# Full 128-row transposes with masked blocks added in PSUM, and new durations in the list schedule's table

## The chip, the cores and the metric

One Trainium2 chip; the kernel runs on one of its cores. The metric is device time in microseconds (us) from the start to the end of one execution; lower is better. Several executions are made, and their median is compared. The engines are named as the profile names them: PE (TensorE matmuls), PEld (the weight loads of TensorE, which stand in a row of their own), DVE (VectorE), ACT (ScalarE), POOL (GpSimd), SP (the engine that issues the DMAs).

## The reference

Sliding-window attention with a linear bias, followed by a feed-forward layer with an unusual gate. Inputs are float32.

```python
# attention: q, k, v are (8 batches, 8 heads, 576 positions, 64)
scores = q @ k.T / sqrt(64)
rel    = pos_q - pos_k
bias   = -slope[head] * abs(rel)
scores = where((rel >= 0) & (rel < 128), scores + bias, -1e9)
attn   = exp(scores - max); attn /= attn.sum() + 1e-9
x      = (attn @ v)  # laid out as (4608 tokens, 512)

# feed-forward: w_in (512, 2048), w_out (2048, 512)
h   = x @ w_in
g   = h * erf(softplus(h))
out = g @ w_out
```

A query sees the 128 keys up to its own position. With key blocks of 64, the queries that see key block b are the 192 from 64b on.

## The kernel before, in words

The work has two halves that run interleaved. **Attention** goes over 32 pairs of heads (8 batches, 4 pairs). **The feed-forward layer**, called MoE in the code, goes over 12 chunks of 384 tokens and 16 slices of 128 hidden features, in two passes: the first pass does 6 slices for all chunks, while attention still makes the tokens, and the second does the other 10, once the memory of attention is free. A float32 product is made of three products of a rounded high part and a remainder (names ending in `h` and `l`).

One pair of heads has five query tiles (`QTILES`, line 56): four of 128 rows, and a last one of 64 rows (queries 512 to 575). For each tile, `scores` (line 472) makes the scores of both heads on PE (line 506), DVE adds the bias with the mask and takes the minimum (line 517), ACT takes the exponential and its sum (line 527); `normalise` (line 536) takes the reciprocal of the sums on DVE (lines 544, 545) and scales the tile on POOL (line 555). The result `p` has queries on partitions and, for each of up to four key blocks, 64 keys of both heads side by side (128 columns). Masked entries are exact zeros there.

The product with v needs keys on partitions, so `transpose_bank` (line 562) transposes blocks of `p` on PE into one PSUM bank (line 574), and ACT or DVE copies the bank to SBUF (lines 468, 470; `pa`, `pb`). `SPANS` (line 61) says which blocks go where: span 0 holds tiles 0 to 2 and has two banks, span 1 holds tiles 3 and 4 and has two more. An entry `(tile, r0, r1, key block)` transposes rows r0 to r1 of one key block. Since key block b is seen by 192 queries, it takes a whole tile (128 rows) and half of a neighbouring one (64 rows): the half with the mask's zeros is left out. So in a bank transposes of 128 and of 64 rows alternate: 128, 64, 128, 64, 128 in the first bank of span 0; 64, 128, 64, 128, 64 in the second; 128, 64 and 64, 64, 128, 64, 64 in those of span 1. That is 17 transposes for a pair of heads and 544 in all. `av` (line 586) then multiplies by v (line 592) into `px`, which goes to SBUF and DRAM as the tokens `x`.

MoE work on PE is line 778 (x by w_in, 384 columns) and line 840 (g by w_out, 512 columns). Lines 807 to 825 and 762, 764 make the gate on ACT, DVE and POOL.

What sets the order of the work: every piece is an `op` with a cost for each engine that may run it and a due time. `Plan.run` is a list scheduler in Python: it plays the whole program through with those costs, gives each engine the ready piece that is due first, chooses between engines where two are allowed (a copy on ACT or DVE, a remainder on DVE or POOL), and writes the instructions out in the order that results. On the chip each engine works through its list in that order. The costs are formulas in the number of columns (`f32r_us`, `fp32_us`, `dve`, `act`, `pool_tt`, `pool_ts`, lines 290 to 311). They set the order, and nothing else.

Of the kernel before, what the change touches and what calls it, by code (L numbers as in the profile page):

```python
# [25 lines left out]
CH = 384  # L26
# [26 lines left out]
W2A, W2B = 60, 2.0  # L53


QTILES = [(128, 2, 4), (128, 0, 4), (128, 0, 4), (128, 0, 4), (64, 0, 3)]

# [3 lines left out]
SPANS = [  # L61
    (
        (0, 1, 2), 0, 384,
        [
            ([(0, 0, 128, 2), (1, 0, 64, 0), (1, 0, 128, 2), (2, 0, 64, 0), (2, 0, 128, 2)], 0, 0),
            ([(0, 64, 128, 3), (1, 0, 128, 1), (1, 64, 128, 3), (2, 0, 128, 1), (2, 64, 128, 3)], 1, 0),
        ],
        {0: (0, 0, 0, 192), 2: (0, 192, 128, 320), 4: (0, 384, 256, 384),
         1: (1, 0, 64, 256), 3: (1, 192, 192, 384), 5: (1, 384, 320, 384)},
        [(0, 3), (1, 2), (4, 5)],  # L70
    ),
    (
        (3, 4), 384, S,
        [
            ([(3, 0, 128, 1), (3, 64, 128, 3)], 0, 0),
            ([(4, 0, 64, 1), (3, 0, 64, 0), (3, 0, 128, 2), (4, 0, 64, 0), (4, 0, 64, 2)], 0, 192),
        ],
        {5: (0, 0, 384, 512), 7: (0, 128, 448, 576), 4: (0, 256, 384, 448),
         6: (0, 320, 384, 576), 8: (0, 512, 512, 576)},
        [(6, 4), (5, 7, 8)],  # L80
    ),
]
SUB = ALU.subtract
# [204 lines left out]


def f32r_us(n):  # L290
    return max(n / 2400.0, 0.091) + 0.0025


def fp32_us(n):
    return max(n / 600.0, 0.191) + 0.0045


def dve(n, fast=False):
    return 0.068 + n * (0.000521 if fast else 0.001042)


def act(n, aps=0, src=0.093):
    return src + 0.093 * aps + n * 0.000833


def pool_tt(n):
    return 0.09 + n * 0.0022


def pool_ts(n):  # L310
    return 0.245 + n * 0.00083
# [27 lines left out]
class Attention:  # L339
# [132 lines left out]
    def scores(self, i, t, operands, low, total, at):  # L472
        nc, op = self.nc, self.plan.op
        g = self.order[i][1]
        m, c0, c1 = QTILES[t]
        n = (c1 - c0) * 64
        a, kh, kl, q0, k0 = operands
        q0 = t * P - q0
        k0 = (2 * t - 2 + c0) * 64 - k0
        src = []  # L480
        if kl is None:

# [6 lines left out]
            def products(e):  # L489
# [22 lines left out]
        pt = Buf(self.pp, [P, 4, 2, 64], F32, "p", PB, f"p{i}_{t}")  # L512
# [16 lines left out]
                    accum_out=total[:m, j : j + 1],  # L529
                )  # L530

        op({"DVE": 2 * dve(n)}, biased, r=list(dict.fromkeys(s[0] for s in src)), w=[pt, low], at=at)
        op({"Act": 2 * act(n, 2)}, exps, r=[pt, low], w=[pt, total], at=at)
        return pt

    def normalise(self, i, ts, p, st, totals, at):

        nc, op = self.nc, self.plan.op
        m = QTILES[ts[0]][0]
        k = [2 * (t % 3) for t in ts]  # L540
        both = lambda: st[:m, 6 + k[0] : 8 + k[-1]]

        def inverse(e):
            nc.vector.tensor_scalar(both(), both(), 1e-9, None, op0=ALU.add)
            nc.vector.reciprocal(both(), both())  # L545

        sums = [totals[t] for t in ts]
        op({"DVE": 0.28}, inverse, r=sums, w=sums, at=at)
        for t in ts:
            _, c0, c1 = QTILES[t]  # L550

            def scaled(e, t=t, c0=c0, c1=c1):
                for j in range(2):
                    dst = p[t][:m, c0:c1, j, :]
                    nc.gpsimd.tensor_scalar(  # L555
                        dst, dst, totals[t][:m, j : j + 1], 1.0, op0=ALU.mult, op1=ALU.mult
                    )

            n = (c1 - c0) * 64
            op({"Pool": 2 * (0.245 + n * 0.00083)}, scaled, r=[p[t], totals[t]], w=[p[t]], at=at)  # L560

    def transpose_bank(self, i, w, bi, p, sb, at):
        nc, op = self.nc, self.plan.op
        parts, sbi, off = SPANS[w][3][bi]
# [4 lines left out]
        width = sum(r1 - r0 for _, r0, r1, _ in parts)  # L569

        def transposes(e):
            col = 0
            for t, r0, r1, kb in parts:
                nc.tensor.transpose(  # L574
                    ps[:, col : col + r1 - r0], p[t][r0:r1, kb].rearrange("p j d -> p (j d)"),
                    self.ident[r0:r1, r0:r1],
                )
                col += r1 - r0

        op({"PE": width / 1200.0 + 0.02}, transposes,  # L580
           r=[p[t] for t in sorted({x[0] for x in parts})], w=[ps], at=at)
        op({"DVE": dve(width), "Act": act(width, src=0.051)},
           lambda e: self.copy(e, sb[sbi][:, off : off + width], ps[:, :width]),
           r=[ps], w=[sb[sbi]], at=at)

    def av(self, i, w, blks, dst, v, sb, at):
# [14 lines left out]
    def span(self, i, w, operands, v):  # L601
        b, g = self.order[i]
        op = self.plan.op
# [30 lines left out]
        op({"DVE": dve(n), "Act": act(n, src=0.051)},  # L634
           lambda e: self.copy(e, xs.all, px[:, :n]), r=[px], w=[xs], at=at + 0.1)
        xd = Part(self.moe.x_dram[c], slice(None), g, slice(off, off + n))
        self.moe.x_parts[c].append(xd)
# [55 lines left out]
class Moe:  # L693
# [72 lines left out]
    def unit(self, c, f, w, x, po, start, end, first, at):  # L766
        nc, op = self.nc, self.plan.op
        U = self.U
        wh, wl = w.t[0, f]
        ps = Buf(self.ps_h, [P, 512], F32, "h", 2, f"h{U}")  # L770
        for k2 in range(2):
            xh, xl = x[k2]

            def products(e, k2=k2, xh=xh, xl=xl):
                for k in range(2):
                    cs = slice((2 * k2 + k) * P, (2 * k2 + k + 1) * P)
                    for n, (ww, xx) in enumerate(((wh, xh), (wh, xl), (wl, xh))):
                        nc.tensor.matmul(  # L778
                            ps[:, :CH], lhsT=ww[:, cs], rhs=xx[:, k],
                            start=(k2 + k + n == 0), stop=(k2 + k + n == 4),  # L780
                        )
# [5 lines left out]
        op({"Act": act(CH, src=0.051), "DVE": dve(CH)},  # L787
           lambda e: self.copy(e, hs[:, half], ps[:, :CH]), r=[ps], w=[hs], at=at)
        return dict(U=U, c=c, f=f, w=w, po=po, start=start, end=end, first=first, hs=hs, at=at)

# [58 lines left out]
    def store(self, u, t, po, at):  # L849
# [114 lines left out]
```

## Time and profile before

| what | value |
|---|---|
| median of 3 executions | 1168.37 us (1168.31 to 1174.0) |
| the profiled execution | 1174.66 us, span 1172.9 us from first to last instruction |
| busy: PE, DVE, ACT, POOL | 97%, 62%, 58%, 33% of the span |
| mean clock granted to TensorE | 0.978 |
| transposes (line 574) | 544, the first at 14.7 us, the last at 572.9 us |

The profile is one execution. A row of a group gives busy time, the mean length of one instruction in ns, and the idle time of the engine ahead of it. A row of the timeline gives the start, the length, the engine and the instructions that were merged into it; since matmuls overlap, the time that one holds PE is the distance from its start to the start of the next, not its length. Shapes are written as rows*columns of the array, then partitions x elements.

### The profile page before, as it was taken

Reading aid. Unit: us, or ns where it says so; the run is one execution under the profiler, and the core shown is the slowest. Engines: PE = TensorE matmul, PEld = TensorE weight load, DVE = VectorE, ACT = ScalarE, POOL = GpSimd, SP = SyncE. Lnnn points to the kernel's source line nnn. Section 1 sums busy time; section 2 is a strip of 40 time slices with the busy share of each in tenths; the row PEclk is TensorE's granted clock in tenths of the full one; section 3 lists DMA queues with packets and bytes.
Section 4 is the critical chain, followed back from the end, with each engine's and each line's share of the span. In section 5 each row is a group of like instructions: output and inputs, shape, how many; then the busy total and the mean of one; then the engine's idle time right before and its main releaser. Section 6 shows DMA issues by size and latency. Waiting matters only on the chain.

```text
span 1172.9 us, 17108 instructions
## 1 busy us (share of the span) xinstructions
PE 1133.4 (97%) x6000; PEld 983.7 (84%) x6000; DVE 723.9 (62%) x1670; ACT 680.9 (58%) x1368; POOL 389.9 (33%) x464
## 2 busy tenths in 40 slices
PE   8997889999999999999999999999999999999998
PEld 6875768888778788887899999899999999999997
DVE  7877999876966686766587877343344234324433
ACT  6556656774776576756557666354455544554552
POOL 6876677636544554553333343000000000000000
PEclk9987989999998999999999999999999999999999
DMA  7443555444434234341133341122022112102102
GB/s 201 125 123 93 149 144 155 136 124 109 125 110 134 71 111 143 102 120 67 65 110 124 126 144 55 54 81 81 1 82 81 33 49 81 57 25 82 54 1 81
DMA packets 89733, 111.61 MB, mean 95 GB/s; under 512 B 45744, under 2 KB 59696, under 8 KB 89648
## 3 DMA queue, kind: packets, MB, share of 16 engines
q1 hardware_dynamic: 89648, 110.52, 31.4%
q8 instruction: 48, 0.79, 0.3%
q14 instruction: 37, 0.30, 0.1%
HBM read 82.18 MB, written 28.31 MB: 94 GB/s over the span
## 4 chain that ended last, share of the span: by engine, by line
PE 48%; DVE 1%; ACT 1%; POOL 1%; issue 0%; POOLq 0%
PE o L840 24%; PE h L778 24%; POOL wto L682 0%; DVE hs L820 0%; DVE wto L671 0%; DVE gl L825 0%; ACT s L807 0%; DVE wqo L674 0%; POOL wlo L688 0%; ACT L807 0%; DVE wqo L673 0%; PE px L592 0%; DVE wto L669 0%; DVE xl L755 0%; DVE gh L764 0%
## 5 line engine op out<-in xcount | busy, mean ns | idle before, releaser
L778 PE MATMUL h<-xh,whi 128*128 128x384 f32 x768 | 264.3, 344 | 0.0
L778 PE MATMUL h<-xh,wli 128*128 128x384 f32 x768 | 261.1, 340 | 0.4 <-POOL wli L688 0.4
L778 PE MATMUL h<-xl,whi 128*128 128x384 f32 x768 | 260.2, 339 | 0.8 <-DVE xl L755 0.8
L555 POOL TENSOR_SCALAR p<-p,st 128x256 f32<-128x256 f32 (+2 forms) x320 | 199.8, 641 | 180.3 <-DVE st L545 128.9
L840 PE MATMUL o<-who,gh 128*128 128x512 f32 x576 | 228.4, 397 | 0.0
L840 PE MATMUL o<-wlo,gh 128*128 128x512 f32 x576 | 227.8, 395 | 0.5 <-POOL wlo L688 0.5
L840 PE MATMUL o<-who,gl 128*128 128x512 f32 x576 | 228.1, 396 | 0.0
L762 ACT COPY hs<-h 128x384 f32<-128x384 f32 x142 | 67.9, 479 | 254.9 <-PE h L778 254.1
L527 ACT ACTIVATE p<-p,st 128x256 f32<-128x256 f32 (+2 forms) x320 | 149.2, 468 | 63.9 <-DVE st L517 62.9
L778 PEld LDWEIGHTS h<-xh,whi 128*128 128x128 f32 x768 | 145.9, 190 | 8.4
L778 PEld LDWEIGHTS h<-xl,whi 128*128 128x128 f32 x768 | 145.7, 190 | 7.8 <-DVE xl L755 1.1
L778 PEld LDWEIGHTS h<-xh,wli 128*128 128x128 f32 x768 | 145.4, 189 | 1.2 <-POOL wli L688 1.2
L574 PE MATMUL t<-ident,p 64*128 64x64 f32 (+1 forms) x544 | 123.7, 290 | 17.5 <-POOL p L555 14.6
L517 DVE CUSTOM_DVE_ANT_0 p<-s,bias_sb 128x256 f32<-128x256 f32 (+2 forms) x320 | 109.0, 377 | 49.0 <-PE s L506 42.1
L764 DVE COPY hs<-h 128x384 f32<-128x384 f32 x50 | 27.8, 556 | 177.2 <-PE h L778 177.0
L574 PEld LDWEIGHTS t<-ident,p 64*128 64x128 f32 (+1 forms) x544 | 72.9, 143 | 74.7 <-POOL p L555 23.0
L840 PEld LDWEIGHTS o<-who,gl 128*128 128x128 f32 x576 | 108.3, 188 | 23.6
L840 PEld LDWEIGHTS o<-who,gh 128*128 128x128 f32 x576 | 109.0, 189 | 16.2 <-DVE ot L860 0.2
L840 PEld LDWEIGHTS o<-wlo,gh 128*128 128x128 f32 x576 | 108.6, 188 | 16.7 <-POOL wlo L688 0.9
L820 DVE TENSOR_TENSOR hs<-s,hs 128x768 f32<-128x768 f32 x96 | 94.6, 1008 | 24.3 <-ACT s L809 24.2
L825 DVE TENSOR_TENSOR gl<-hs,gh 128x768 fp32r<-128x768 f32 x96 | 99.3, 1052 | 1.5 <-ACT gh L762 1.4
L462 POOL TENSOR_TENSOR a_None<-qr_None,a_None 64x576 fp32r<-64x576 f32 x48 | 77.0, 1605 | 35.3 <-DVE a_None L470 20.4
(80 smaller groups left out, 1632.4 us busy)
## 6 DMA issues: line engine op xcount, KB each, us to landing
xr<-xd SPq DMA_DIRECT2D x22, 768.0 KB, 4.3
kr_None<-k_t SPq DMA_DIRECT2D x48, 288.0 KB, 4.1
pd<-ot SPq DMA_DIRECT2D x36, 256.0 KB, 4.1
ot<-pd SPq DMA_DIRECT2D x36, 256.0 KB, 2.9
wri<-w_in SPq DMA_DIRECT2D x16, 512.0 KB, 4.4
wro<-w_out SPq DMA_DIRECT2D x16, 512.0 KB, 3.5
out_dram<-ot SPq DMA_DIRECT2D x32, 256.0 KB, 2.1
qr_None<-q_t SPq DMA_DIRECT2D x24, 288.0 KB, 3.8
```

The source lines that it names most:

```text
L462: op({"Pool": pool_tt(nq)}, lambda e, j=j, own=own, other=other: nc.gpsimd.tensor_tensor(a[j][other, :nq], q[own, :nq], a[j][own, :nq], SU ...
L517: nc.vector.tensor_tensor_reduce(out=pt[:m, c0:c1, j, :], in0=blocks(src[j][0][:m, src[j][1], :n]), in1=blocks(self.bias[:m, c0 * 64 : c1 ...
L527: nc.scalar.activation(dst, dst, AF.Exp, bias=low[:m, j : j + 1], scale=-1.0, accum_out=total[:m, j : j + 1],)
L555: nc.gpsimd.tensor_scalar(dst, dst, totals[t][:m, j : j + 1], 1.0, op0=ALU.mult, op1=ALU.mult)
L574: nc.tensor.transpose(ps[:, col : col + r1 - r0], p[t][r0:r1, kb].rearrange("p j d -> p (j d)"), self.ident[r0:r1, r0:r1],)
L762: self.nc.scalar.copy(out, src)
L764: self.nc.vector.tensor_copy(out, src)
L778: nc.tensor.matmul(ps[:, :CH], lhsT=ww[:, cs], rhs=xx[:, k], start=(k2 + k + n == 0), stop=(k2 + k + n == 4),)
L820: V if e == "DVE" else G).tensor_tensor(hs[:, :n], s[:, :n], hs[:, :n], ALU.mult),
L825: V if e == "DVE" else G).tensor_tensor(gl[:, :n], hs[:, :n], gh[:, :n], SUB),
L840: nc.tensor.matmul(po.all, lhsT=g[:, j, cs], rhs=w.all, start=(u["start"] and n == 0), stop=(u["end"] and n == 2),)
```

## The change

1. All query tiles have 128 rows. The last one now covers queries 448 to 575; its first 64 rows repeat queries of tile 3, and are computed again.
2. Every transpose takes 128 rows. Where a key block needs a whole tile and half of the next one, the whole next tile is transposed too, half of it being zeros of the mask, and where two of these overlap in the bank the second is added to the first in PSUM (`start=False`): zeros are added to values. The number of transposes stays 17 for a pair of heads: 5, 5, 5 and 2 in the four banks. The first bank of span 1 now takes blocks of tiles 3 and 4 (before of tile 3 alone), the second too.
3. The copies out of the banks keep their widths (512, 448, and 384 and 192), and the products with v keep their number and widths; the blocks lie at other columns and come in another order.
4. The cost formulas get other numbers, so the list scheduler writes another order for every engine, and makes other choices between engines.

```diff
-QTILES = [(128, 2, 4), (128, 0, 4), (128, 0, 4), (128, 0, 4), (64, 0, 3)]
+QTILES = [(0, 2, 4), (128, 0, 4), (256, 0, 4), (384, 0, 4), (448, 1, 4)]
...
-            ([(0, 0, 128, 2), (1, 0, 64, 0), (1, 0, 128, 2), (2, 0, 64, 0), (2, 0, 128, 2)], 0, 0),
+            ([(0, 2, 0, 0), (1, 0, 128, 0), (1, 3, 128, 1), (2, 1, 256, 0), (2, 2, 384, 0)], 0, 512, 0, 0),
...
-            ([(3, 0, 128, 1), (3, 64, 128, 3)], 0, 0),
+            ([(4, 2, 64, 0), (3, 0, 0, 0), (3, 3, 0, 1), (4, 1, 256, 0), (3, 2, 192, 0)], 0, 384, 0, 0),
...
 def f32r_us(n):
-    return max(n / 2400.0, 0.091) + 0.0025
+    return max(n / 2400.0 + 0.0135, 0.11)
...
-def act(n, aps=0, src=0.093):
+def act(n, aps=0, src=0.15):
...
-    return 0.245 + n * 0.00083
+    return 0.36 + n * 0.00135
...
         def transposes(e):
-            col = 0
-            for t, r0, r1, kb in parts:
-                nc.tensor.transpose(
-                    ps[:, col : col + r1 - r0], p[t][r0:r1, kb].rearrange("p j d -> p (j d)"),
-                    self.ident[r0:r1, r0:r1],
+            for n, (t, kb, col, added) in enumerate(parts):
+                nc.tensor.matmul(
+                    ps[:, col : col + P], lhsT=p[t][:, kb].rearrange("p j d -> p (j d)"),
+                    rhs=self.ident[:, :], is_transpose=True, start=not added,
+                    stop=(n + 1 == len(parts) or not parts[n + 1][3]),
                 )
-                col += r1 - r0
-
-        op({"PE": width / 1200.0 + 0.02}, transposes,
+
+        op({"PE": 0.1 * len(parts) + 0.02}, transposes,
...
-           lambda e: self.copy(e, sb[sbi][:, off : off + width], ps[:, :width]),
+           lambda e: self.copy(e, sb[sbi][:, off : off + width], ps[:, c0:c1]),
```

What moves, shown at pair 10 of the 32. In the names, `t10_0_0` is the bank of pair 10, span 0, number 0; `p10_1` is tile 1 of that pair; `px10_0` is its product with v; `s11_1` are scores of the next pair; `o` and `h` are MoE. Line numbers after the change are higher by 4 or 5.

The first place is PE, the first bank of span 0, before:

```order
L574 MATMUL t10_0_0_2358<-ident_62,p10_0_2184 128x128
L574 MATMUL t10_0_0_2358<-ident_62,p10_1_2217 128x64
L574 MATMUL t10_0_0_2358<-ident_62,p10_1_2217 128x128
L574 MATMUL t10_0_0_2358<-ident_62,p10_2_2263 128x64
L574 MATMUL t10_0_0_2358<-ident_62,p10_2_2263 128x128
L840 MATMUL o1_6_2147<-who2_1755,gh8_2092 128x512
```

And after, the same bank:

```order
L578 MATMUL t10_0_0_2346<-ident_62,p10_0_2153 128x128
L578 MATMUL t10_0_0_2346<-ident_62,p10_1_2205 128x128 x2
L578 MATMUL t10_0_0_2346<-ident_62,p10_2_2240 128x128 x2
L844 MATMUL o1_6_2200<-who2_1817,gh8_2198 128x512
L844 MATMUL o1_6_2200<-wlo2_1823,gh8_2198 128x512
```

Five transposes stand there in both, and the two of 64 columns have become 128 wide; the bank has the same MoE work behind it.

The second place is PE, up to the first bank of span 1; before, four products for `s11_1` and six for `h15` stand between the second bank of span 0 and these rows, which begin with the last of the six:

```order
L778 MATMUL h15_2406<-xh2_0_2018,wli3_1071 128x384
L592 MATMUL px10_0_2418<-pa10_0_2369,vbd0_160 128x192
L592 MATMUL px10_0_2418<-pa10_1_2404,vbd0_160 128x192 x2
L592 MATMUL px10_0_2418<-pa10_0_2369,vbd0_160 128x192
L592 MATMUL px10_0_2418<-pa10_0_2369,vbd0_160 128x128
L592 MATMUL px10_0_2418<-pa10_1_2404,vbd0_160 128x64
L574 MATMUL t10_1_0_2433<-ident_62,p10_3_2296 128x128
L574 MATMUL t10_1_0_2433<-ident_62,p10_3_2296 128x64
```

And after, from the end of the second bank of span 0:

```order
L578 MATMUL t10_0_1_2374<-ident_62,p10_2_2240 128x128 x2
L596 MATMUL px10_0_2386<-pa10_0_2365,vbd0_160 128x192 x2
L596 MATMUL px10_0_2386<-pa10_0_2365,vbd0_160 128x128
L596 MATMUL px10_0_2386<-pa10_1_2390,vbd0_160 128x192 x2
L596 MATMUL px10_0_2386<-pa10_1_2390,vbd0_160 128x64
L578 MATMUL t10_1_0_2400<-ident_62,p10_4_2312 128x128
L578 MATMUL t10_1_0_2400<-ident_62,p10_3_2283 128x128 x2
L578 MATMUL t10_1_0_2400<-ident_62,p10_4_2312 128x128
L578 MATMUL t10_1_0_2400<-ident_62,p10_3_2283 128x128
L511 MATMUL s11_1_2408<-kh11_None_0_2115,a11_None_0_2128 128x256
```

The products for `s11_1` and `h15`, which stood ahead of the product with v, now stand behind the first bank of span 1, and that bank begins with tile 4.

The third place is POOL, the scaling of tiles 3 and 4 of the same pair, on which that bank waits, before:

```order
L555 TENSOR_SCALAR p10_2_2263<-p10_2_2263,st10_0_2185 128x4x64 x2
L555 TENSOR_SCALAR p10_3_2296<-p10_3_2296,st10_1_2297 128x4x64 x2
L462 TENSOR_TENSOR a12_None_0_2327<-qr12_None_2226,a12_None_0_2327 64x576
L555 TENSOR_SCALAR p10_4_2335<-p10_4_2335,st10_1_2297 64x3x64 x2
L462 TENSOR_TENSOR a12_None_1_2354<-qr12_None_2226,a12_None_1_2354 64x576
```

And after:

```order
L560 TENSOR_SCALAR p10_2_2240<-p10_2_2240,st10_0_2154 128x4x64 x2
L560 TENSOR_SCALAR p10_3_2283<-p10_3_2283,st10_1_2284 128x4x64 x2
L560 TENSOR_SCALAR p10_4_2312<-p10_4_2312,st10_1_2284 128x3x64 x2
L466 TENSOR_TENSOR a12_None_0_2330<-qr12_None_2258,a12_None_0_2330 64x576
L466 TENSOR_TENSOR a12_None_1_2354<-qr12_None_2258,a12_None_1_2354 64x576
```

The scaling of tile 4 now stands ahead of a remainder for pair 12 that stood between the two.

More of the change, by code (lines that the diff above doesn't have):

```diff
@@ L74 @@
         [
-            ([(3, 0, 128, 1), (3, 64, 128, 3)], 0, 0),
-            ([(4, 0, 64, 1), (3, 0, 64, 0), (3, 0, 128, 2), (4, 0, 64, 0), (4, 0, 64, 2)], 0, 192),
-        ],
-        {5: (0, 0, 384, 512), 7: (0, 128, 448, 576), 4: (0, 256, 384, 448),
-         6: (0, 320, 384, 576), 8: (0, 512, 512, 576)},
-        [(6, 4), (5, 7, 8)],
+            ([(4, 2, 64, 0), (3, 0, 0, 0), (3, 3, 0, 1), (4, 1, 256, 0), (3, 2, 192, 0)], 0, 384, 0, 0),
+            ([(4, 3, 64, 0), (3, 1, 0, 0)], 0, 192, 0, 384),
+        ],
+        {4: (0, 0, 384, 448), 7: (0, 64, 448, 576), 6: (0, 192, 384, 576),
+         5: (0, 384, 384, 512), 8: (0, 512, 512, 576)},
+        [(6, 4, 7), (5, 8)],
     ),
@@ L474, in scores @@
         g = self.order[i][1]
-        m, c0, c1 = QTILES[t]
+        m = P
+        start, c0, c1 = QTILES[t]
         n = (c1 - c0) * 64
         a, kh, kl, q0, k0 = operands
-        q0 = t * P - q0
-        k0 = (2 * t - 2 + c0) * 64 - k0
+        k0 = start - WIN + c0 * 64 - k0
+        q0 = start - q0
         src = []
@@ L530, in exps @@
                 )
-        op({"DVE": 2 * dve(n)}, biased, r=list(dict.fromkeys(s[0] for s in src)), w=[pt, low], at=at)
-        op({"Act": 2 * act(n, 2)}, exps, r=[pt, low], w=[pt, total], at=at)
+        op({"DVE": 2 * (dve(n) + 0.08)}, biased, r=list(dict.fromkeys(s[0] for s in src)), w=[pt, low], at=at)
+        op({"Act": 2 * (act(n, 1) + 0.19)}, exps, r=[pt, low], w=[pt, total], at=at)
         return pt
@@ L538, in normalise @@
         nc, op = self.nc, self.plan.op
-        m = QTILES[ts[0]][0]
+        m = P
         k = [2 * (t % 3) for t in ts]
@@ L547, in normalise @@
         sums = [totals[t] for t in ts]
-        op({"DVE": 0.28}, inverse, r=sums, w=sums, at=at)
+        op({"DVE": 0.5}, inverse, r=sums, w=sums, at=at)
         for t in ts:
@@ L559, in normalise @@
             n = (c1 - c0) * 64
-            op({"Pool": 2 * (0.245 + n * 0.00083)}, scaled, r=[p[t], totals[t]], w=[p[t]], at=at)
+            op({"Pool": 2 * pool_ts(n)}, scaled, r=[p[t], totals[t]], w=[p[t]], at=at)
     def transpose_bank(self, i, w, bi, p, sb, at):
         nc, op = self.nc, self.plan.op
-        parts, sbi, off = SPANS[w][3][bi]
+        parts, c0, c1, sbi, off = SPANS[w][3][bi]
         if i < NPAIR and w == 0 and bi % 2:
@@ L568, in transpose_bank @@
             ps = Buf(self.ps, [P, 512], F32, "t", 1, f"t{i}_{w}_{bi}")
-        width = sum(r1 - r0 for _, r0, r1, _ in parts)
+        width = c1 - c0
         def transposes(e):
-            col = 0
-            for t, r0, r1, kb in parts:
-                nc.tensor.transpose(
-                    ps[:, col : col + r1 - r0], p[t][r0:r1, kb].rearrange("p j d -> p (j d)"),
-                    self.ident[r0:r1, r0:r1],
-                )
-                col += r1 - r0
-        op({"PE": width / 1200.0 + 0.02}, transposes,
+            for n, (t, kb, col, added) in enumerate(parts):
[3 more added lines that the diff above has]
+                    stop=(n + 1 == len(parts) or not parts[n + 1][3]),
+                )
+        op({"PE": 0.1 * len(parts) + 0.02}, transposes,
            r=[p[t] for t in sorted({x[0] for x in parts})], w=[ps], at=at)
-        op({"DVE": dve(width), "Act": act(width, src=0.051)},
-           lambda e: self.copy(e, sb[sbi][:, off : off + width], ps[:, :width]),
+        op({"DVE": dve(width), "Act": act(width, src=0.13)},
+           lambda e: self.copy(e, sb[sbi][:, off : off + width], ps[:, c0:c1]),
            r=[ps], w=[sb[sbi]], at=at)
@@ L633, in span @@
             xs = Buf(self.xsb, [P, n], F32, f"xs{w}", 1, f"xs{i}_{w}")
-        op({"DVE": dve(n), "Act": act(n, src=0.051)},
+        op({"DVE": dve(n), "Act": act(n, src=0.13)},
            lambda e: self.copy(e, xs.all, px[:, :n]), r=[px], w=[xs], at=at + 0.1)
@@ L786, in unit @@
         hs, half = self.hs, len(self.round) % 2
-        op({"Act": act(CH, src=0.051), "DVE": dve(CH)},
+        op({"Act": act(CH, src=0.13), "DVE": dve(CH)},
            lambda e: self.copy(e, hs[:, half], ps[:, :CH]), r=[ps], w=[hs], at=at)
@@ L854, in store @@
         if u["first"]:
-            op({"DVE": dve(DM), "Act": act(DM, src=0.051)},
+            op({"DVE": dve(DM), "Act": act(DM, src=0.13)},
                lambda e: self.copy(e, ot.all, po.all), r=[po], w=[ot], at=at)
```

14 lines of the change are left out of this document (7 added, 7 removed).

## The prediction

> **What bounds the kernel now.** First the page: how busy each engine is over the whole span.
>
> ```profile
> span 1172.9 us, 17108 instructions
> PE 1133.4 (97%) x6000; PEld 983.7 (84%) x6000; DVE 723.9 (62%) x1670; ACT 680.9 (58%) x1368; POOL 389.9 (33%) x464
> ```
>
> PE is the bound on average. An average says nothing of a stage, so next the windows, cut at 200 us and at the last transpose, once for all instructions and once for line 574 alone (with the row that tells its first and last start). The columns are length, then busy time and count of PE, PEld, DVE, ACT and POOL, then the granted clock.
>
> ```profile
> 0.00:200.00 200.00, 176.24 (x945) 144.96 (x946) 168.41 (x482) 121.34 (x335) 141.14 (x172) 0.89 0.51 141
> 200.00:573.00 373.00, 362.60 (x2079) 301.47 (x2077) 264.08 (x794) 249.02 (x643) 193.48 (x255) 0.99 0.38 109
> 573.00:1172.90 599.90, 594.61 (x2979) 537.28 (x2977) 291.44 (x395) 310.56 (x392) 55.29 (x38) 1.00 0.21 71
> ```
>
> ```profile
> L574 PE MATMUL t<-ident,p x544: 221/273/477, 14.7 to 572.9; 64*128 64x64 f32 x106, 128*128 128x128 f32 x76
> 0.00:200.00 200.00, 40.21 (x170) 23.47 (x170) 0.89 0.51 141
> 200.00:573.00 373.00, 83.37 (x374) 49.41 (x374) 0.99 0.38 109
> ```
>
> Three stages. Up to 200 us PE stands 23.8 us, its clock is 0.89, and DVE is busy for 168 of 200 us: PE is not alone in setting the pace. From 200 to 573 us PE stands only 10.4 us and no other engine is over 71%: what is taken off PE there comes off the end. After 573 us there is only MoE work on a full PE, which the change doesn't shorten. At 17 transposes for a pair, 10 pairs lie in the first stage and 22 in the second.
>
> Last the timeline, for what a transpose costs PE. These are the four banks of pair 10 with their neighbours; the time a bank holds PE is from its start to the start of the next row.
>
> ```profile
> 200.39 1.22 PE L574 MATMUL t<-ident,p 128*128 128x128 f32 x5
> 201.37 0.48 PE L840 MATMUL o<-who,gh 128*128 128x512 f32 x1
> 202.38 0.39 PE L840 MATMUL o<-wlo,gh 128*128 128x512 f32 x1
> 202.60 0.39 PE L840 MATMUL o<-who,gl 128*128 128x512 f32 x1
> 202.92 1.20 PE L574 MATMUL t<-ident,p 64*128 64x64 f32 x5
> 204.05 0.39 PE L506 MATMUL s<-kh_None,a_None 128*128 128x256 f32 x1
> 205.16 0.33 PE L778 MATMUL h<-xh,whi 128*128 128x384 f32 x1
> 205.33 0.33 PE L778 MATMUL h<-xl,whi 128*128 128x384 f32 x1
> 207.36 0.48 PE L574 MATMUL t<-ident,p 128*128 128x128 f32 x2
> 207.77 0.38 PE L506 MATMUL s<-kh_None,a_None 128*128 128x256 f32 x1
> 208.11 0.28 PE L506 MATMUL s<-kh_None,a_None 128*128 128x256 f32 x1
> 208.23 0.28 PE L506 MATMUL s<-kl_None,a_None 128*128 128x256 f32 x1
> 208.44 0.86 PE L574 MATMUL t<-ident,p 64*128 64x64 f32 x5
> 209.23 0.44 PE L778 MATMUL h<-xh,whi 128*128 128x384 f32 x1
> ```
>
> The banks hold PE 0.98, 1.13, 0.41 and 0.79 us, 3.31 us together. A bank that begins with 64 rows also starts late: 202.60 to 202.92 is 0.32 where the product ahead took 0.22, and 208.23 to 208.44 is 0.21 where it took 0.12, so 0.09 twice or more, 0.18. **One pair pays 3.49 us for its 17 transposes**, 0.205 each. Check: 22 pairs times 3.31 is 73; the window has 83 because the record of a bank's last transpose runs on over the next instruction (201.29 and 0.33, against 201.37).
>
> Why so much, the weight loads beside the matmuls show, in narrow cuts of the first and the last of these banks:
>
> ```profile
> 200.62 0.53 PE L574 MATMUL t<-ident,p 64*128 64x64 f32 x2
> 200.62 0.14 PEld L574 LDWEIGHTS t<-ident,p 64*128 64x128 f32 x1
> 201.09 0.53 PE L574 MATMUL t<-ident,p 64*128 64x64 f32 x2
> 201.29 0.33 PE L574 MATMUL t<-ident,p 128*128 128x128 f32 x1
> 208.44 0.33 PE L574 MATMUL t<-ident,p 64*128 64x64 f32 x2
> 208.55 0.48 PE L574 MATMUL t<-ident,p 64*128 64x64 f32 x2
> 208.44 0.20 PEld L574 LDWEIGHTS t<-ident,p 64*128 64x128 f32 x2
> ```
>
> The second transpose of the first bank (64 rows after 128) has its load at 200.62 and its matmul at 200.62: the load did not go ahead under the transpose before, which had begun at 200.39. From there 0.23 passes for one transpose of 128 rows, and 0.20 for one of 64 (201.09 to 201.29). Where two of 64 rows follow each other, at 208.44, the second load runs under the first matmul (two loads of 0.14 in 0.20 us, so the second began at 208.50) and the matmuls are 0.11 apart. And the last transpose of a bank, with 128 rows, at 201.29, gives PE to the next full product at 201.37, after 0.08. So what is paid for is the change of shape, not the transpose.
>
> **The change part by part.** *Shape.* No transpose now differs in shape from its neighbours or from the MoE products. The trace has no two full transposes in a row. From below the price is 0.08 (the one at 201.29), from above 0.20 (what one costs today where loads are not hidden). I take 0.11 inside a bank, by the two equal neighbours at 208.44, and 0.08 for the last of each bank: 13 × 0.11 + 4 × 0.08 = 1.75 us, and 1.74 us saved for a pair. The half that is zeros adds columns, but the 128-column transpose at 201.29 shows them to fit in 0.08. In the second stage 22 × 1.74 = 38.3 us comes off PE and off the end. In the first, 10 × 1.74 = 17.4 us comes off PE, but PE stands there and DVE is at 84%; I count half, 8.7, between none and all. Sum: 47 us. With 0.08 throughout and all of the first stage it is 32 × (3.49 − 1.36) = 68; with 0.20, 32 × 0.09 = 3.
>
> The Trainium skill, "TensorE: Matmul & The Clock Gate", Part 3, says that a weight load overlaps matmuls in flight only when the row groups differ. By that, full transposes would each wait for their load, at 0.205 as now, and nothing would be saved. The trace disagrees at 208.50, where a load for rows 0 to 63 runs under a matmul on rows 0 to 63. In Part 4 the same page gives about 275 ns for a transpose of 128 by 128 in a kernel; 17 × 0.275 = 4.7 us for a pair would be an estimate of 38 us lost.
>
> *The last tile's 64 more rows.* Scores, bias, exponential and scaling keep their 192 columns. Exponentials of other shapes on ACT:
>
> ```profile
> 196.90 0.51 ACT L527 ACTIVATE p<-p,st 128x256 f32<-128x256 f32 x1 [0.74 <-DVE st L517]
> 199.96 0.44 ACT L527 ACTIVATE p<-p,st 64x192 f32<-64x192 f32 x1
> 203.72 0.40 ACT L527 ACTIVATE p<-p,st 128x128 f32<-128x128 f32 x1 [1.05 <-DVE st L517]
> ```
>
> 64 rows of 192 columns lie midway between 128 rows of 128 and of 256, so columns set the length, not rows: nothing. If a doubling of rows did cost 0.05 us on each of these engines, ACT's and DVE's free time (below) would hide it in the second stage. *Adding in PSUM and the new order of the products with v*: same counts and widths, nothing.
>
> *The order.* Two things to weigh. First, work goes from DVE to ACT: the program now has 13 more `kh` scalings, 11 more `a` casts and 6 more `xh` casts on ACT, and 9 more `pa` copies, nearly all in the first two stages, at such lengths:
>
> ```profile
> L449 ACT ACTIVATE kh_None<-kr_None 128x576 fp32r<-128x576 f32 x17 | 11.5, 681 | 1.2 <-DMA kr_None<-k_t 0.8 <-PE s L506 0.4
> L468 ACT CAST a_None<-qr_None 64x576 fp32r<-64x576 f32 x17 | 11.4, 670 | 3.1 <-DMA qr_None<-q_t 2.7 <-PE s L506 0.2
> ```
>
> Some 39 × 0.68 = 26 us. ACT has 370 us of work up to 573 (121 + 249); 396 in some 526 us would be 75%. DVE has 432 and loses about 20: 412 of 526, 78%. Neither becomes the bound on average. Second, the waits of PE for tiles, whose largest are:
>
> ```profile
> PEld t L574 <- POOL p L555: 23.0, 33, 4.1
> PE t L574 <- POOL p L555: 14.6, 17, 3.9
> ```
>
> And what an exponential takes, with the reading of its sum:
>
> ```profile
> L527 ACT ACTIVATE p<-p,st 128x256 f32<-128x256 f32 (+2 forms) x320 | 149.2, 468 | 63.9 <-DVE st L517 62.9
> L527 ACT ACTIVATION_READ_ACCUMULATOR p<-p,st 128x1 f32 (+1 forms) x320 | 60.1, 188 | 0.0
> ```
>
> The old table's costs were too short against this (two exponentials of 256 columns stood at 2 × 0.49 us, and these groups have 0.66 for one), so the old order sends PE to tiles that are not ready; the new one should send it later. On the other side, the first bank of span 1 now waits for tile 4 as well, and the products that stood ahead of it are behind it. What such a bank would meet can be worked out for pair 10:
>
> ```profile
> 201.40 1.81 POOL L462 TENSOR_TENSOR a_None<-qr_None,a_None 64x576 fp32r<-64x576 f32 x1
> 203.60 0.98 POOL L555 TENSOR_SCALAR p<-p,st 64x192 f32<-64x192 f32 x2 [0.39 <-DVE st L545]
> ```
>
> Tile 4 is scaled by 204.58 and PE came to that bank at 207.36, 2.8 us later. After the change PE comes earlier by the ten products moved (four of 0.12, and six of 0.17 as from 205.16 to 205.33: 1.5) and by the 1.2 saved in the two banks of span 0, 2.7 in all; POOL does tile 4 ahead of the 1.81 of the remainder, so about 2 us earlier. Some 2 us of cover are left, 0.1 or less if the remainder's place brings nothing. I put the order at a gain of 3 us, with bounds of −20 (most of what PE stands before 573 us, 34 us) and +14 (0.44 us more for each pair at this bank).
>
> Total: 47 + 3 = 50 us. The profiled execution, 1174.66, would become 1124.7; it lies 6.3 above the median of the three runs shown, on which the same 50 gives **1118 us**.
>
> **The rivals.** *A, the above*, 1104 to 1132: 0.52. *B, other engines take up half.* DVE is at 84% in the first stage, and as PE shortens, copies of banks and exponentials come late in their queues. For: DVE's 168 of 200. Against: no engine over 71% in the second stage. The gain is 25, 1143. 0.17. *C, the order brings its full bound too.* Half of the first stage's loss comes back with it, as the clock of 0.89 rises: 47 + 8.7 + 20 = 76, 1092. For: 23.8 us of standing, and 0.11 of 176 us lost to the clock. Against: the first stage has DVE. 0.17. *D, loads of full transposes are not hidden*, 0.20 each: 3 us, 1165. Against it stand the loads at 208.50 and the 0.08 at 201.29. 0.06. *E, PE stands at the first bank of span 1* waiting for POOL's tile 4, with everything behind it in its list, the next pair's scores included, so that DVE, ACT and POOL get that tile late in turn. To be slower than before by over 6 us it must cost 56 us, 1.75 us in each of 32 pairs beyond what the waits above cost now; at pair 10 that is reached if POOL is nearly 4 us later than worked out. 3 us a pair gives 1168 − 50 + 96 = 1214. For: 37.6 us of such waits now, up to 4.1 long. Against: cover of 2 us. 0.06. *F, a full transpose holds PE for its whole record*, 0.33 as at 201.29: 17 × 0.33 = 5.6, 2.1 more for a pair, 67 more, 1235. Against: the next product began after 0.08. 0.02. The 275 ns of the Trainium skill (Part 4, above) would be of this kind.
>
> **How the numbers follow.** A measurement of this kernel can tell about 0.5%, 6 us, from no change; that puts the border at 1162.5. A, B and C are below it: 0.86 faster. D is within: 0.06. E and F: 0.08 slower. For 8 in 10 the range takes A, most of B and most of C: 1088 to 1150, by the bounds of the order (−20, +14) and of the price of a transpose.
>
> **What would show it.** In the new profile, line 578 (the transposes) should have 544 instructions of one shape, five of them 0.5 to 0.55 us apart from start to next, and busy time of 55 to 75 us in place of 123.6 (40.2 + 83.4). The last transpose should come at about 525 us in place of 572.9, with about 600 us behind it as now. PE's standing up to there should stay near 34 us, the wait of transposes for POOL near 38 us. The forecast is wrong if five full transposes still take about 1 us (D), if ACT or DVE stand above 90% in the second stage with PE waiting (B), or if `t` waits for POOL have grown beyond 90 us (E).

## The result, and the profile after

| | before | after |
|---|---|---|
| median, beside each other on one chip | 1171.18 us | 1118.55 us |
| ratio, with its 95% interval | | 0.9546 (0.9508 to 0.9583) |
| the profiled execution, and its span | 1174.66, 1172.9 | 1118.25, 1116.3 |

A second set of runs of the changed kernel, on another chip, had 1118.09 us and 0.9518 (0.9493 to 0.9543). The kernel is 4.5 to 5% faster: 53 us, where 50 were forecast, and the forecast of 1118 us for the median is met. Two executions took two to three times as long as the others (2389 us of the kernel before, 3486 us of `e3_alternate`); the ratios leave them out, and without it the median of `e3_alternate`, given below as 1145.47 us, is 1144.88 us.

The page after, and its windows cut at the last transpose; the columns are as before (length, then PE, PEld, DVE, ACT and POOL busy, then the clock):

```profile
span 1116.3 us, 17069 instructions
PE 1073.7 (96%) x6000; PEld 976.5 (87%) x6000; DVE 684.9 (61%) x1602; ACT 721.9 (65%) x1436; POOL 385.7 (35%) x464
```

```profile
0.00:200.00 200.00, 168.67 (x1012) 151.86 (x1013) 162.57 (x479) 135.87 (x370) 145.06 (x177) 0.91 0.53 148
200.00:525.00 325.00, 320.01 (x2069) 297.30 (x2068) 251.49 (x764) 255.90 (x650) 186.72 (x249) 1.00 0.45 126
525.00:1116.00 591.00, 585.00 (x2923) 527.38 (x2921) 270.82 (x360) 330.17 (x417) 53.89 (x38) 1.00 0.21 70
```

PE is busy for 59.7 us less and the span is 56.6 us shorter. The stage with attention has shrunk; in its second part (200 to 525 us) PE stands 5.0 us in 325, before 10.4 in 373. In the first 200 us PE stands more than before, 31.3 us against 23.8.

The transposes, as a group, with their first and last start:

```profile
L578 PE MATMUL t<-ident,p 128*128 128x128 f32 x544 | 85.7, 284 | 17.6 <-POOL p L560 11.8 <-ACT pb L472 2.8 <-ACT pa L472 1.6
L578 PE MATMUL t<-ident,p x544: 270/273/477, 16.6 to 520.0; 128*128 128x128 f32 x182
```

One shape is left, and the last transpose comes at 520.0 us, 52.9 earlier than before; behind it 596 us pass, before 600. So nearly the whole gain, 52.9 of 56.6 us, lies ahead of the last transpose, as the prediction had it. The four banks of pair 10 again, with what follows each, and a narrow cut of the first bank's weight loads:

```profile
190.77 0.40 PE L844 MATMUL o<-who,gl 128*128 128x512 f32 x1
191.00 0.71 PE L578 MATMUL t<-ident,p 128*128 128x128 f32 x5
191.47 0.48 PE L844 MATMUL o<-who,gh 128*128 128x512 f32 x1
191.78 0.39 PE L844 MATMUL o<-wlo,gh 128*128 128x512 f32 x1
192.01 0.39 PE L844 MATMUL o<-who,gl 128*128 128x512 f32 x1
192.71 0.39 PE L844 MATMUL o<-who,gl 128*128 128x512 f32 x1
192.94 0.71 PE L578 MATMUL t<-ident,p 128*128 128x128 f32 x5
193.48 1.87 PE L596 MATMUL px<-pa,vbd 128*128 128x192 f32 x12
195.19 0.72 PE L578 MATMUL t<-ident,p 128*128 128x128 f32 x5
195.66 0.36 PE L511 MATMUL s<-kh_None,a_None 128*128 128x256 f32 x1
197.27 0.38 PE L578 MATMUL t<-ident,p 128*128 128x128 f32 x2
197.41 0.42 PE L782 MATMUL h<-xh,whi 128*128 128x384 f32 x1
```

```profile
191.00 0.25 PEld L578 LDWEIGHTS t<-ident,p 128*128 128x128 f32 x2
191.11 0.38 PE L578 MATMUL t<-ident,p 128*128 128x128 f32 x2
```

From start to the next row the banks hold PE 0.47, 0.54, 0.47 and 0.14 us: 1.62 us for the pair, before 3.49. (Both sums are a little low, because the product behind a bank is slowed as well; the part on the prediction comes back to it.) The first bank starts 0.23 after the product ahead of it, which is that product's own time: nothing is lost at the entry. Two loads of 0.14 stand in 0.25 us from 191.00, so the second began at 191.11, together with the matmul ahead of its own: the load of each transpose runs under the transpose before it. That matmul of 191.11 is the second of the bank, 0.11 after the first.

### The profile page after: what moved, and what is told of

Its sections match the earlier page's. It is cut to its first block, busy times and chain, and to the rows that moved or that the text cites. A ratio compares the mean times of both kernels' runs of the same rounds, so it can differ in the third digit from the quotient of the medians.

```text
span 1116.3 us, 17069 instructions
## 1 busy us (share of the span) xinstructions
PE 1073.7 (96%) x6000; PEld 976.5 (87%) x6000; DVE 684.9 (61%) x1602; ACT 721.9 (65%) x1436; POOL 385.7 (35%) x464
## 4 chain that ended last, share of the span: by engine, by line
PE 82%; DVE 9%; POOL 3%; DMA 2%; issue 2%; ACT 2%; POOLq 0%; SPq 0%; DVEq 0%; ACTq 0%
PE o L844 32%; PE h L782 31%; PE px L596 7%; PE s L511 5%; PE t L578 5%; POOL p L560 2%; DMA xr<-xd 2%; DVE p L522 1%; PE warm_ps L383 1%; DVE xl L759 1%; POOL wto L686 1%; DVE hs L824 1%; DVE gl L829 1%; PE s L497 1%; ACT p L532 1%
## 5 line engine op out<-in xcount | busy, mean ns | idle before, releaser
L560 POOL TENSOR_SCALAR p<-p,st 128x256 f32<-128x256 f32 (+2 forms) x320 | 194.0, 623 | 128.1 <-DVE st L550 108.1
L766 ACT COPY hs<-h 128x384 f32<-128x384 f32 x137 | 65.3, 477 | 215.1 <-PE h L782 214.6
L768 DVE COPY hs<-h 128x384 f32<-128x384 f32 x55 | 30.4, 554 | 160.8 <-PE h L782 160.8
L829 DVE TENSOR_TENSOR gl<-hs,gh 128x768 fp32r<-128x768 f32 x96 | 94.6, 989 | 15.5 <-ACT gh L766 14.7
L578 PE MATMUL t<-ident,p 128*128 128x128 f32 x544 | 85.7, 284 | 17.6 <-POOL p L560 11.8
L578 PEld LDWEIGHTS t<-ident,p 128*128 128x128 f32 x544 | 65.6, 147 | 30.4 <-POOL p L560 14.6
L466 POOL TENSOR_TENSOR a_None<-qr_None,a_None 64x576 fp32r<-64x576 f32 x48 | 76.4, 1592 | 25.7 <-DVE a_None L474 20.7
```

What stands on the lines that cost most here:

```text
L466: op({"Pool": pool_tt(nq)}, lambda e, j=j, own=own, other=other: nc.gpsimd.tensor_tensor(a[j][other, :nq], q[own, :nq], a[j][own, :nq], SU ...
L560: nc.gpsimd.tensor_scalar(dst, dst, totals[t][:m, j : j + 1], 1.0, op0=ALU.mult, op1=ALU.mult)
L578: nc.tensor.matmul(ps[:, col : col + P], lhsT=p[t][:, kb].rearrange("p j d -> p (j d)"), rhs=self.ident[:, :], is_transpose=True, start=no ...
L766: self.nc.scalar.copy(out, src)
L829: V if e == "DVE" else G).tensor_tensor(gl[:, :n], hs[:, :n], gh[:, :n], SUB),
```

## The experiments

Ten more kernels were run, and the changed kernel a second time, each beside the kernel before; ratios carry a 95% interval. Theory S is the prediction's: the change of shape is what a transpose pays for. Theory O is its rival: the new order made the gain. "Order" stands for all that the cost table decides, the sequence on each engine and the choices between engines; no run here separates these two.

### The two halves of the change, apart

`e1_shape` has the new tiles, banks and full transposes, with the old cost table. Its edit, against the changed kernel:

```diff
 def f32r_us(n):
-    return max(n / 2400.0 + 0.0135, 0.11)
+    return max(n / 2400.0, 0.091) + 0.0025
...
-            op({"Pool": 2 * pool_ts(n)}, scaled, r=[p[t], totals[t]], w=[p[t]], at=at)
+            op({"Pool": 2 * (0.245 + n * 0.00083)}, scaled, r=[p[t], totals[t]], w=[p[t]], at=at)
...
-        op({"PE": 0.1 * len(parts) + 0.02}, transposes,
+        op({"PE": P * len(parts) / 1200.0 + 0.02}, transposes,
```

> The new tiles and full transposes, with the old cost table (the transposes' own cost kept at 128 columns each by the old formula). Theory S, what is paid for is the change of shape: 47 us come off as in the changed kernel, about 1124 us against 1171. Theory O, the new order made most of the gain: 1150 us or more.

`e2_order` has the old tiles and mixed transposes, with the new cost table:

```diff
 def f32r_us(n):
-    return max(n / 2400.0, 0.091) + 0.0025
+    return max(n / 2400.0 + 0.0135, 0.11)
...
-        op({"PE": width / 1200.0 + 0.02}, transposes,
+        op({"PE": 0.2 * len(parts) + 0.02}, transposes,
```

> The old tiles and transposes of 128 and 64 rows, with the new cost table (the transposes' own cost at 0.2 us each, as the trace of before has it). S: within 6 us of before, 1165 to 1177. O: 1125 to 1140 us.

| kernel | median | ratio to before |
|---|---|---|
| full transposes, old costs (`e1_shape`) | 1155.84 us | 0.9844 (0.9817 to 0.9871) |
| mixed transposes, new costs (`e2_order`) | 1163.33 us | 0.9903 (0.9873 to 0.9933) |
| both | 1118.55 us | 0.9546 (0.9508 to 0.9583) |

Neither S nor O is right by itself (`e1_shape` lies in O's range, `e2_order` just below S's): 17 us come from the shape alone (1173.22 to 1155.84), 10 from the order alone (1173.22 to 1163.33), and both together give 53. The two parts need each other. Why the shape alone gives so little, the page of `e1_shape` and its waits show (the columns are total us, times, and the longest):

```profile
span 1152.2 us, 17073 instructions
PE 1077.8 (94%) x6000; PEld 973.0 (84%) x6000; DVE 709.3 (62%) x1659; ACT 688.3 (60%) x1379; POOL 391.4 (34%) x464
```

```profile
PE t L578 <- POOL p L560: 30.9, 28, 4.9
PE s L511 <- DVE st L522: 19.7, 25, 3.8
```

PE's busy time fell by 55.6 us (1133.4 to 1077.8), nearly as in the changed kernel, but the span only by 20.7: PE stands 74 us in place of 40. Transposes wait for POOL's scaled tiles 30.9 us, before 14.6, and scores for DVE 19.7 us, before 11.4. The same rows of the changed kernel:

```profile
PE s L511 <- DVE st L522: 12.5, 13, 2.0
PE t L578 <- POOL p L560: 11.8, 7, 5.4
```

So the old order sends a faster PE to tiles that are not ready, and what the transposes give is spent there.

### Which entry of the cost table does it

`e6_pool_cost` is `e1_shape` with one entry set to the profile:

```diff
-            op({"Pool": 2 * (0.245 + n * 0.00083)}, scaled, r=[p[t], totals[t]], w=[p[t]], at=at)
+            op({"Pool": 2 * (0.36 + n * 0.00135)}, scaled, r=[p[t], totals[t]], w=[p[t]], at=at)
```

> New tiles and full transposes with the old cost table as in e1_shape, and one entry set to the profile, POOL's scaling (2 x 0.71 us for 256 columns in place of 2 x 0.46). Theory P, the wait of transposes for POOL, which grew to 31 us in e1_shape, is what eats the gain there and this entry causes it: 1125 to 1135. Theory C, all entries of the chain from scores to scaling must be right together: 1145 to 1156.

`e7_chain_costs` sets the rest of the chain as well:

```diff
-        op({"DVE": 2 * dve(n)}, biased, r=list(dict.fromkeys(s[0] for s in src)), w=[pt, low], at=at)
-        op({"Act": 2 * act(n, 2)}, exps, r=[pt, low], w=[pt, total], at=at)
+        op({"DVE": 2 * (0.25 + n * 0.00108)}, biased, r=list(dict.fromkeys(s[0] for s in src)), w=[pt, low], at=at)
+        op({"Act": 2 * (0.433 + n * 0.000833)}, exps, r=[pt, low], w=[pt, total], at=at)
...
-        op({"DVE": 0.28}, inverse, r=sums, w=sums, at=at)
+        op({"DVE": 0.5}, inverse, r=sums, w=sums, at=at)
```

> As e6_pool_cost, with the entries of bias, exponential and reciprocal set to the profile too; MoE, weights, copies and operands keep the old ones. C: 1118 to 1130. P: as e6_pool_cost. If the rest of the table matters as much: 1135 to 1145.

`after_again` is the changed kernel, run beside them:

> The changed kernel once more, beside the runs that are compared with it: 1116 to 1120 us, 0.955 of before.

| kernel | median | ratio to before |
|---|---|---|
| `e6_pool_cost` | 1136.19 us | 0.9677 (0.9648 to 0.9706) |
| `e7_chain_costs` | 1129.76 us | 0.9622 (0.9592 to 0.9652) |
| `after_again` | 1118.09 us | 0.9518 (0.9493 to 0.9543) |

In `e6_pool_cost` the waits are:

```profile
PE s L511 <- DVE st L522: 25.8, 33, 2.3
...
PE t L578 <- POOL p L560: 2.7, 4, 1.1
```

One number in the scheduler's table, POOL's 0.46 us for a scaling of 256 columns that takes about 0.7 (four take 2.93 us at pair 10 of the changed kernel, shown below), is worth some 20 of the 38 us between `e1_shape` and the changed kernel. It does what theory P said, and its result lies just above P's 1125 to 1135; PE stands 54 us in its profile (1133.7 less 1080.1), where it stood 74 in `e1_shape`: the transposes' wait for POOL goes from 30.9 to 2.7 us, and part of it comes back one step earlier, where scores now wait 25.8 us for DVE. The chain's other entries bring 6 more, to the upper end of theory C's range (1118 to 1130). How they do it is open: in the trace of `e7_chain_costs` PE stands no less (57 us), and transposes wait 12.1 us for POOL again. The last 12 lie in the rest of the table (copies, operands, weights, MoE), which was not taken apart.

### The price of the change of shape, with the order held

`e3_alternate` keeps the changed kernel's order on every engine (but for the order of the transposes inside a bank) and its 17 transposes, but takes 64 rows where the other half is zeros, in 5 of the 17, and adds nothing; its results are the same:

```diff
-            for n, (t, kb, col, added) in enumerate(parts):
-                nc.tensor.matmul(
-                    ps[:, col : col + P], lhsT=p[t][:, kb].rearrange("p j d -> p (j d)"),
-                    rhs=self.ident[:, :], is_transpose=True, start=not added,
-                    stop=(n + 1 == len(parts) or not parts[n + 1][3]),
+            halves = ((0, 64), (64, 128), (0, 64), (64, 128))[2 * w + bi]
+            for x in ((0, 2, 1, 3, 4), (0, 3, 4, 1, 2), (0, 2, 1, 3, 4), (0, 1))[2 * w + bi]:
+                t, kb, col, _ = parts[x]
+                r0, r1 = halves if kb == (3 if halves[0] else 0) else (0, P)
+                nc.tensor.transpose(
+                    ps[:, col + r0 : col + r1], p[t][r0:r1, kb].rearrange("p j d -> p (j d)"),
+                    self.ident[r0:r1, r0:r1],
                 )
```

> The changed kernel with the same order on every engine and the same 17 transposes for a pair, but 5 of the 17 take 64 rows where the other half is zeros, so fewer columns pass and nothing is added. S: each of the three 64-row ones between full ones costs 0.22 us more, the two at a bank's start 0.18, about 1.0 us a pair: 33 us if all shows, 27 with half of the first ten pairs, so 1145 to 1152. O, or a price that goes by columns: 1118 or a little less.

Measured: 1145.47 us, 0.9742 (0.9716 to 0.9768). That is the lower end of S's 1145 to 1152. The first bank of pair 10 there has one transpose of 64 rows in five:

```profile
197.65 0.95 PE L581 MATMUL t<-ident,p 128*128 128x128 f32 x5
198.35 0.47 PE L846 MATMUL o<-who,gh 128*128 128x512 f32 x1
```

It holds PE 0.70 us, and 0.47 with five full ones: 0.23 for one 64-row transpose between full ones, where 0.22 was expected. Over its four banks pair 10 pays 1.2 us more than in the changed kernel (2.65 us from start to next row where that had 1.62, and 0.09 at each of two late starts), which would be 39 us in 32 pairs. With order, count and results alike and fewer columns passing, 27 us are lost. That is the price of a change of shape, shown directly, for 5 transposes of a pair; the kernel before has 10 with 64 rows.

### What PE's time is worth in each stage

`e4_twice_first` issues every bank's transposes twice in the first 10 pairs, `e5_twice_rest` in the other 22; the order stays and the result too, since the second set writes the same again:

```diff
-            for n, (t, kb, col, added) in enumerate(parts):
-                nc.tensor.matmul(
+            for again in range(2 if i < 10 else 1):
+                for n, (t, kb, col, added) in enumerate(parts):
+                    nc.tensor.matmul(
...
```

(`i >= 10` in the other.)

> The changed kernel, same order, with every bank's transposes issued twice in the first 10 pairs alone, 170 more at 0.11 us, 18.7 us of PE time. If the first stage hides half, as predicted: 9 us longer, 1128. If PE is the bound there: 19 us, 1137. If other engines set the pace there: 0 to 3 us.

> The changed kernel, same order, with every bank's transposes issued twice in pairs 10 to 31, 374 more at 0.11 us, 41 us of PE time. If PE is the bound from there on, as predicted: 41 us longer, about 1160. If other engines set the pace there as in the first ten pairs, where twice cost 3 us of 19: 7 us, 1126.

`e4_twice_first` took 1121.81 us, 0.9557 (0.9538 to 0.9577); `e5_twice_rest` 1154.34 us, 0.9826 (0.9795 to 0.9856). In the second stage 374 more transposes at 0.11, 41 us of PE time, cost 36 us: PE is the bound there, or nearly. In the first stage 18.7 us cost some 3 to 4 by the medians (1118.09 and 1118.55 against 1121.81), and the intervals of the ratios overlap. The windows of `e4_twice_first`, first stage and second, show where the rest went:

```profile
0.00:200.00 200.00, 173.49 (x1131) 158.22 (x1132) 157.79 (x471) 132.43 (x359) 140.97 (x175) 0.94 0.50 140
200.00:525.00 325.00, 320.04 (x2080) 297.94 (x2079) 256.28 (x771) 257.98 (x658) 192.12 (x252) 1.00 0.45 127
```

PE stands 26.5 us in the first 200, in place of 31.3, and the clock is 0.94 in place of 0.91. So part of the added time fills time in which PE stood. The clock's share is not settled: a second trace of the changed kernel (`after_again`) has 0.93 there, with 32.4 us of standing.

The trace also puts the price higher than the medians do. The first bank of pair 10, with the same other work on PE ahead of it, starts in `after_again` and in `e4_twice_first` at

```profile
190.22 0.71 PE L578 MATMUL t<-ident,p 128*128 128x128 f32 x5
197.99 0.71 PE L579 MATMUL t<-ident,p 128*128 128x128 f32 x5
```

and in the first trace of the changed kernel at 191.00. That is 7 to 8 us of the 18.7, in an execution that was the longest of its four (1124.41 us). Between a fifth and two fifths of PE's added time shows.

### What sets the pace of the first ten pairs

Two kernels take work off one engine there, in the preparation of the first six slices of weights, with the order unchanged. `e8_dve_light` lets three of DVE's steps take 8 columns in place of 512; `e9_pool_light` does the same with POOL's addition. Both leave out that part of the weights.

```diff
+        c = 8 if f < NF1 else DM
...
-                t.all, q.all, -(1 << 31), t.all, op0=ALU.bitwise_and, op1=ALU.bitwise_or)),
+                t[:, :c], q[:, :c], -(1 << 31), t[:, :c], op0=ALU.bitwise_and, op1=ALU.bitwise_or)),
```

```diff
+        c = 8 if f < NF1 else DM
...
-        op({"Pool": pool_tt(DM)}, lambda e: nc.gpsimd.tensor_tensor(flt(t), flt(t), flt(q), ALU.add),
+        op({"Pool": pool_tt(DM)}, lambda e: nc.gpsimd.tensor_tensor(flt(t)[:, :c], flt(t)[:, :c], flt(q)[:, :c], ALU.add),
```

> The changed kernel, same order; for the six slices of weights prepared in the first stage, three of DVE's steps take 8 columns in place of 512 (the weights come out wrong), about 2.1 us less on DVE for each of 12, 25 us. Theory D, DVE sets the pace of the first ten pairs: they end 10 us or more earlier, and the kernel takes 1105 to 1110. Theory L, the waits come from the length of the chain and from POOL, not from DVE's load: 1115 to 1119.

> The changed kernel, same order; for the same weights POOL's addition takes 8 columns in place of 512 (the weights come out wrong), about 1.3 us less on POOL for each of 12, 16 us, and each weight is ready earlier. If POOL's load sets the pace of the first ten pairs: 8 us or more off, 1110 or less. If DVE does: within 3 us of the changed kernel.

Measured: 1109.93 us, 0.9443 (0.9423 to 0.9464), and 1111.54 us, 0.9462 (0.9444 to 0.9479): 8 and 7 us off the 1118.09 of `after_again`. The first bank of pair 10 starts, with DVE lighter and with POOL lighter, at

```profile
182.17 0.71 PE L578 MATMUL t<-ident,p 128*128 128x128 f32 x5
183.95 0.71 PE L578 MATMUL t<-ident,p 128*128 128x128 f32 x5
```

in place of 190.22 and 191.00, so the gain lies in the first ten pairs. Theory D's 1105 to 1110 is met for DVE, though the pairs end 8 to 9 us earlier and not 10 or more. The result for POOL lies between its two ranges. Its relief is smaller, 16 us against 25, and brings nearly as much; neither engine sets the pace alone. With DVE lighter its window reads:

```profile
0.00:200.00 200.00, 174.08 (x1062) 157.75 (x1063) 155.37 (x504) 144.45 (x383) 141.93 (x179) 0.92 0.54 153
```

PE gets 50 instructions further in 200 us (1062 against 1012). This fits one chain through the weights, DVE, POOL and the tiles, in which any shorter link brings the next forward; the chain itself is argued, not shown link by link.

These two point to a version that spreads the weights' due times. `e10_spread` is that:

```diff
-W1A, W1B, W1C = 12, 4, 0.3
+W1A, W1B, W1C = 12, 4, 0.7
```

> The changed kernel with one due time changed: the six slices of weights for the first pass are due 0.7 of a unit apart in place of 0.3, so that their work on DVE and POOL is spread over more of the first stage. If their crowding there delays the first pairs: 3 to 6 us off, 1112 to 1115. If only their sum matters, and MoE work then lacks weights: within 2 us of 1118, or worse.

It took 1121.09 us, 0.9568 (0.9527 to 0.9609): not faster than the changed kernel. The first ten pairs did end earlier, as hoped for:

```profile
186.65 0.71 PE L578 MATMUL t<-ident,p 128*128 128x128 f32 x5
```

That is 4 us ahead of the changed kernel's 190.22 and 191.00. But the last transpose comes at 522.5 us in place of 520.0, so 6 to 7 us are lost between; PE stands 9.3 us between 200 and 525, where it stood 5.0. Why is not shown. None of the kernels that do all of the work is faster than the changed kernel.

## Why the prediction was right, and where its steps were not

**The price of a transpose: right inside a bank, too low at its end.** Forecast 1.75 us for a pair, measured 1.62 at pair 10 by starts, from 3.49. Inside a bank the matmuls are 0.11 apart, as the two equal 64-row neighbours of the trace before had it. The last of a bank was taken at 0.08, since the next product started 0.08 after the one at 201.29; now it starts 0.03 after the fifth. Both readings miss that this product holds PE longer than its like. In the trace before it is followed by

```profile
201.69 0.40 PE L840 MATMUL o<-wlo,gh 128*128 128x512 f32 x1
201.92 0.39 PE L840 MATMUL o<-who,gl 128*128 128x512 f32 x1
```

so it held PE 0.32 (201.37 to 201.69) where the next held 0.23; after, 0.31 (191.47 to 191.78) and 0.23. Only the product with v, behind the second bank, is not slowed, and there the five transposes hold 0.54, 0.11 each. With this counted at the other banks (0.08 to 0.11 each) pair 10 pays 1.87 us, 17 times 0.11, from 3.89. So 2.0 us are saved for a pair where 1.74 were forecast, and the prediction's lower bound of 0.08 for a full transpose is not what the trace shows. The sentence of the Trainium skill ("TensorE: Matmul & The Clock Gate", Part 3) that loads overlap only where row groups differ, which would have left nothing to save, fails again at 191.11; so do rivals D and F.

**The check by busy time: wrong in size.** It was to be 55 to 75 us and is 85.7, though PE is held less than forecast. The records of a bank's last transposes run on over the next instruction (191.00 and 0.71, against 191.47), and there are 128 banks. Starts come nearer to what PE is held for than lengths do.

**"In the second stage 38.3 us comes off PE and off the end": right only with the new order.** The step took it that PE's time goes to the end of the kernel as before, whatever the order. `e1_shape` shows that with the old order most of it turns into waits: PE busy 55.6 us less, 17 us gained. `e5_twice_rest` and `e3_alternate` show that with the new order PE's time does go to the end, at 36 us for 41 in the second stage, and in both stages together at 27 for the 39 that pair 10 makes of it (33 were expected at most). For the changed kernel as a whole the balance is the one assumed: PE is busy 59.7 us less and stands 42.6 us in place of 39.5.

**"I put the order at a gain of 3 us, with bounds of −20 and +14": the term that was mis-sized.** With the new transposes the order is worth 38 us (1155.84 to 1118), beyond its bound; with the old ones 10. The prediction named the mechanism (costs too short, PE sent to tiles that are not ready) but priced it by how PE stood before, 34 us, and not by how it would stand once it were faster. The sum came out because the term for the shape counted as gained what only the order could deliver: 17 + 38 is near 47 + 3. That the new order brought PE's standing up to the last transpose back to where it had been (36.3 us, before 34.2) was assumed and not worked out, so the nearness of the total is in part luck. Rival C had the order at its bound, but on top of a full gain from the shape; the standing of the first stage did not come back.

**"In the first I count half": not settled as a number.** Of 18.7 us of PE time added there, about a fifth shows by the medians of `e4_twice_first` and two fifths at pair 10 of its trace. In `e3_alternate` pair 10 starts at 197.65, 7 us later than in the changed kernel, for 12 us that its ten pairs pay: more than half. Against the kernel before, the first bank of pair 10 comes 9.4 us earlier (191.00 against 200.39), near the 8.7 counted, but the new order has its part in that. That DVE at 84% holds this stage was half of the truth, as POOL does so too (`e8_dve_light`, `e9_pool_light`).

**Rival E, waiting for tile 4: not there.** POOL's list at pair 10 after the change, tiles 0 to 2, then 3 and 4, then the remainders:

```profile
186.10 3.23 POOL L560 TENSOR_SCALAR p<-p,st 128x128 f32<-128x128 f32 x6 [2.22 <-DVE st L550]
189.74 2.93 POOL L560 TENSOR_SCALAR p<-p,st 128x256 f32<-128x256 f32 x4 [0.42 <-DVE st L550]
192.76 3.27 POOL L466 TENSOR_TENSOR a_None<-qr_None,a_None 64x576 fp32r<-64x576 f32 x2
```

Tile 4 is done at 192.67 and PE comes to the bank at 195.19: 2.5 us of cover, where some 2 were worked out. In the whole kernel PE's and PEld's waits of transposes for POOL went from 37.6 to 26.4 us (32.4 in the second trace of the changed kernel), where they were to stay near 38; a wait of PEld and one of PE can cover the same stretch:

```profile
PEld t L578 <- POOL p L560: 14.6, 10, 5.5
PE t L578 <- POOL p L560: 11.8, 7, 5.4
```

**Rival B: not there.** ACT has 392 us of work up to 525 us (135.87 + 255.90), 75%, as forecast, and DVE 414 (162.57 + 251.49), 79%, where 78% was; both are busier than before in the second stage and PE stands less. **The last tile's 64 more rows cost nothing**, as forecast; the exponentials' mean is the same 468 ns (bias 377 before and 378 after, scaling 641 and 623):

```profile
L532 ACT ACTIVATE p<-p,st 128x256 f32<-128x256 f32 (+2 forms) x320 | 149.0, 468 | 24.5 <-DVE st L522 23.6
```

## What to carry to other kernels

Small matmuls of alternating shape can cost more than full ones that do twice the work: before packing less work into a matmul, look in the trace whether its weight load still runs under its neighbour (0.11 us a transpose if so, 0.20 to 0.23 if not). When a static order is built from a table of durations, taking time off the busiest engine pays in full only if the table is right for the engines that feed it; here the old table left 17 us of a gain of 53, and one entry that was a third too short accounts for 20 of the rest. To learn whether an engine's time is worth anything in a stage, double a cheap piece of its work there: 41 us of it cost 36 in one stage here, and 19 cost between 4 and 8 in another.

## What the runs showed of the hardware that was not expected

The granted clock was a little higher when transposes were added in the first stage. Over the four runs each, the mean clock was 0.983, 0.987, 0.983 and 0.985 for the changed kernel, 0.985 to 0.987 in its second set, and 0.988, 0.994, 0.992 and 0.992 with the first ten pairs' transposes twice. With those of the other 22 pairs twice, where the clock is 1.00 anyhow, it was 0.982 to 0.987. The Trainium skill, "TensorE: Matmul & The Clock Gate", Part 4, says that transposes don't count as activity for the clock in the way that other matmuls do. The runs don't settle whether they count: the added ones also shift all other work of that stage, and `e10_spread`, with none added, has 0.94 over its first 200 us too.

A matmul that follows a full transpose, with rounded operands, starts 0.03 us after it (the fifth transpose of the bank at 191.00, with the next product at 191.47), where one after a full transpose in a mixed bank started after 0.08 (201.29 to 201.37 in the trace before). In both it then holds PE 0.08 to 0.09 longer than its like, so the early start is no sign of a cheap transpose. The same is seen behind the products with v, whose operands are not rounded either: a score product of 256 columns right behind one holds PE 0.20 us in the trace after (median of 17 past 200 us), where one behind another score product holds 0.12. So the slowing goes with the step from unrounded to rounded operands, and not with transposes as such; no run here varied it.
